# The seven products of the first MLP product in another order

## The chip, the cores and the metric

The kernel runs on one core of a Trainium2 chip. The metric is the device time of one execution in microseconds, as the median of repeated runs. The profile is one more execution, recorded by the hardware profiler; its times count from the start of its span.

## The reference

Inputs are q, k, v of shape (8 batches, 8 heads, 576 tokens, 64) and two MLP weights, all float32 at the interface. First comes attention inside chunks of 64 tokens, then a mixing block over the 512 features of each token:

```python
x   = attention(q, k, v)                  # (8, 576, 512), softmax within chunks of 64 tokens
mix = real(fft(fft(x, axis=1), axis=2))   # Fourier mixing over tokens and features
u   = x + mix
un  = (u - mean(u)) / sqrt(var(u) + 1e-6)
out = u + relu(un @ w_ch1) @ w_ch2        # w_ch1: 512 x 2048, w_ch2: 2048 x 512
```

The two matrix products of the last line are the MLP, and most of the work.

## The kernel before, in words

**Tiling.** Tokens are cut into tiles of 128 and the tiles into nine groups of four (512 tokens): one group for each batch, and a last one for the tokens left over. For each group the MLP runs two stages: the first product (512 features to 2048) with a ReLU, into the buffer `h1`, and the second product (2048 back to 512). Attention, Fourier mixing and normalization for the groups to come are cut into steps, and a loop at the end of the kernel (from line 1190) draws some of these steps each time the MLP yields. So the work of other stages stands between the matmuls of the MLP, on all engines.

**The order is written out.** All of it runs under a manual schedule: on each engine the instructions stand in the order in which the Python code issues them. Each engine works through its own queue in that order. If one waits, everything behind it waits.

**Seven products instead of eight.** From group 2 on, `up_halves` (line 998) computes the first product by a Strassen-Winograd scheme: operands are cut into quarters, and seven products of quarter size replace eight. The 2048 outputs are 16 row blocks of 128; block m of the upper half goes with block HF + m of the lower half (HF = 8). The loop takes two such m at once, a pair of row blocks (r = 0, 1), so a group has four pairs. A pair takes seven turns, one for each product `o`. A turn does product `o` for r = 0 and then for r = 1, with two contraction blocks for each: four matmuls of 128 x 128 weights by 256 columns, each of which shows as two records in the trace. With seven such groups that makes 7 x 4 x 7 x 8 = 1568 records on line 1015. The weights of a turn are one slab of 256 KB, fetched from device memory into a ring of ten slabs; `fetch(1)` asks for one more after each turn.

**Where the products go.** For each row block there are two PSUM tiles, `pa` and `pb`, of 2 x 256 float32 per partition, which is 2 KB: a bank each. They come from the pool `ps_f` with four buffers, so the two row blocks of a pair use all four and the next pair uses the same four again. The products of a row block are put together like this, where P0 to P6 are the products by their index `o`, and `a` and `b` are small buffers in `tmp`:

- P0 into `pa`, first half; ScalarE copies it to `a` (line 1020)
- P1 into `pa`, second half; VectorE makes b = P1 + a (line 1022)
- P2 into `pb`, first half; VectorE makes a = P2 + b (line 1024)
- P3 into `pb`, second half; VectorE writes P3 + a to `h1` (line 1026)
- P4 is accumulated onto P0 in `pa`; ScalarE writes its ReLU to `h1` (line 1030)
- P5 is accumulated onto P2 in `pb`; VectorE adds b (line 1032), ScalarE takes the ReLU (line 1033)
- P6 is accumulated onto P3 in `pb`; VectorE adds b (line 1035), ScalarE takes the ReLU (line 1036)

Indices in this text start at 0. The short name of the change counts differently: the product that it calls P6 is P1 here, the one with `o` = 1.

A matmul that is the first into a fresh bank carries the start flag; the first product into the other half of that bank does not, and the accumulating ones don't either.

**Beside the products.** After P3, `operands` (line 917) prepares sums of the previous pair's outputs for the second product: two VectorE instructions (lines 919 and 920) and one of GpSimd (line 921) for each row block. The function yields after turns 1, 3, 5 and 6 of a pair, and there the loop may put in steps of attention: the exponential and the transpose of q (line 348), the transposes of the probabilities on TensorE (line 329) with that of k on VectorE, or the two small attention products (lines 428 and 380) with the softmax on VectorE (lines 441 to 445, 393 and 395). The loads of q and k for the next tile are issued on the SP queue (line 194), the same queue that issues the slabs (line 910) and the small copies of line 481 to 485.

**The second product** (`down_halves`, line 1043) follows the same scheme with longer products: eight contraction blocks for each product and row block.

Of the kernel before, what the change touches and what calls it, by code (L numbers as in the profile page):

```python
# [11 lines left out]
ALU = mybir.AluOpType  # L12
# [4 lines left out]
def kernel(  # L17
# [32 lines left out]
    nc = tc.nc  # L50
# [46 lines left out]


    NO, HF = 7, KF // 2
    s1 = dram.tile([HF // 2, NO, 128, 2 * 2 * 128], FP32, name="s1")  # L100
    s2 = dram.tile([NO, 128, HF * HM], FP32, name="s2")
    NS1, NS2, Z1, Z2 = 10, 3, 2 * 2 * 128, HF * HM
    slab1 = [wa[:, i * Z1:(i + 1) * Z1].rearrange("p (k r f) -> p k r f", r=2, k=2) for i in range(NS1)]
# [58 lines left out]
    start = one_p.tile([128, KF * 512], FP32, tag="big", name="start")  # L162
# [740 lines left out]
    first_of = {1: 2, 2: 1}  # L903
    n_slab = {1: 0, 2: 0}

    def fetch(which):
        i = n_slab[which]
        if which == 1 and i < HF // 2 * NO * (NG - first_of[1]):
            pair, o = divmod(i % (HF // 2 * NO), NO)
            nc.sync.dma_start(out=slab1[i % NS1].rearrange("p k r f -> p (k r f)"), in_=s1[pair, o])  # L910
        elif which == 2 and i < NO * (NG - first_of[2]):
            nc.sync.dma_start(out=slab2[i % NS2].rearrange("p m e -> p (m e)"), in_=s2[i % NO])
        n_slab[which] = i + 1
# [3 lines left out]
    def operands(h1, m):  # L917

        nc.vector.tensor_tensor(out=xs[:, m], in0=h1[:, m, hi], in1=h1[:, HF + m, hi], op=ALU.add)
        nc.vector.tensor_tensor(out=ys[:, m], in0=xs[:, m], in1=h1[:, m, lo], op=ALU.subtract)  # L920
        nc.gpsimd.tensor_tensor(out=h1[:, m, hi], in0=h1[:, m, lo], in1=h1[:, m, hi], op=ALU.subtract)  # L921
# [76 lines left out]
    def up_halves(g):  # L998
        unT = unTs.pop(g)
        h1 = one_p.tile([128, KF, G * 128], FP32, tag="big", name="h1")  # L1000
        rhs = (unT[:, 0:2, lo], tt[:, 1], tt[:, 0], unT[:, 0:2, hi], unT[:, 2:4, lo], unT[:, 2:4, hi], tt[:, 2])
        for pair in range(HF // 2):
            pas, pbs = {}, {}
            for o in range(NO):
                w = slab1[((g - first_of[1]) * HF // 2 * NO + pair * NO + o) % NS1]
                for r in range(2):
                    m = 2 * pair + r
                    a, b = tmp[:, r, 0], tmp[:, r, 1]
                    if o == 0:
                        pas[r] = ps_f.tile([128, 2, 256], FP32, tag="ff", name="pa")  # L1010
                    if o == 2:
                        pbs[r] = ps_f.tile([128, 2, 256], FP32, tag="ff", name="pb")
                    dst = (pas, pas, pbs, pbs, pas, pbs, pbs)[o][r][:, (0, 1, 0, 1, 0, 0, 1)[o]]
                    for kk in range(2):
                        nc.tensor.matmul(  # L1015
                            out=dst, lhsT=w[:, kk, r], rhs=rhs[o][:, kk],
                            start=(o in (0, 2) and kk == 0), stop=(kk == 1), skip_group_check=True,
                        )
                    if o == 0:
                        nc.scalar.copy(a, dst)  # L1020
                    elif o == 1:
                        nc.vector.tensor_tensor(out=b, in0=dst, in1=a, op=ALU.add)  # L1022
                    elif o == 2:
                        nc.vector.tensor_tensor(out=a, in0=dst, in1=b, op=ALU.add)  # L1024
                    elif o == 3:
                        nc.vector.tensor_tensor(out=h1[:, HF + m, hi], in0=dst, in1=a, op=ALU.add)
                        if pair > 0:
                            operands(h1, m - 2)
                    elif o == 4:
                        nc.scalar.activation(out=h1[:, m, lo], in_=dst, func=ACTF.Relu)  # L1030
                    elif o == 5:
                        nc.vector.tensor_tensor(out=h1[:, m, hi], in0=dst, in1=b, op=ALU.add)  # L1032
                        nc.scalar.activation(out=h1[:, m, hi], in_=h1[:, m, hi], func=ACTF.Relu)
                    else:
                        nc.vector.tensor_tensor(out=h1[:, HF + m, lo], in0=dst, in1=b, op=ALU.add)
                        nc.scalar.activation(out=h1[:, HF + m], in_=h1[:, HF + m], func=ACTF.Relu)
                fetch(1)
                if o in (1, 3, 5, 6):
                    yield h1
        for m in (HF - 2, HF - 1):  # L1040
            operands(h1, m)

    def down_halves(g, h1):
        pas, pbs = {}, {}
        for o in range(NO):
            w = slab2[((g - first_of[2]) * NO + o) % NS2]
            for r in range(2):
# [45 lines left out]
                if r == 1:  # L1093
                    if o == 1:
                        for j in range(0, HF, 2):
                            two = ys[:, j:j + 2]
                            nc.gpsimd.tensor_tensor(
                                out=two, in0=h1[:, HF + j:HF + j + 2, lo], in1=two, op=ALU.subtract
                            )
                    if o == 2:  # L1100
                        for i in range(2):
                            nc.gpsimd.tensor_tensor(
                                out=os_[:, 2 * i + 1, HM:DM], in0=tmp[:, i, 0],
                                in1=natural(groups[g][2 + i])[:, HM:DM], op=ALU.add,
                            )
                    fetch(2)
                yield

    def mlp(g):

        for h1 in up_halves(g) if g >= first_of[1] else up_plain(g) if g > 0 else up_first():
            yield
        yield from (down_halves if g >= first_of[2] else down_plain)(g, h1)

    with tc.manual_schedule():
# [74 lines left out]
        for g in range(NG):  # L1190
            for _ in mlp(g):
# [27 lines left out]
                if t == begin[1] + KF // 2:  # L1219
                    for _ in range(NS2):  # L1220
                        fetch(2)
# [52 lines left out]
```

## Time and profile before

| what | value |
|---|---|
| time, median of 3 runs | 1102.69 us (1102.44 to 1103.81) |
| span of the profiled execution | 1100.7 us, granted TensorE clock 0.999 |
| first product by seven products, seven groups, from start to end | 57.3, 57.1, 57.3, 56.5, 54.9, 48.5, 48.5 us |
| of VectorE's time in these stages, busy | 0.64, 0.69, 0.64, 0.70, 0.60, 0.47, 0.47 |

The stages are those between the first and the last record of line 1015 in each group; in the first five, attention and Fourier steps for later groups stand between the products.

A row of groups reads: line, engine, operation, what is written and what is read, shapes, how many; then after a bar the busy time in us and the mean duration of one in ns; then after a second bar the idle time of the engine just before these instructions, and what ended most of it. A row of waits reads: engine, tile and line that waited, what it waited for, then the total in us, how often, and the longest. A row of the timeline reads: start in us, length in us, engine, line, operation, tiles, shapes, number of instructions merged, and in brackets the idle time before the first of them, with what ended it. PE is TensorE, DVE VectorE, ACT ScalarE, POOL GpSimd; SPq is the queue of the SP engine, which issues most transfers.

Matmuls are pipelined, and their records overlap: one record is longer than the distance from its start to the start of the next. To see how fast TensorE goes, compare starts.

### The profile page before, as it was taken

Reading aid. Unit: us, or ns where it says so; the run is one execution under the profiler, and the core shown is the slowest. Engines: PE = TensorE matmul, PEld = TensorE weight load, DVE = VectorE, ACT = ScalarE, POOL = GpSimd, SP = SyncE. Lnnn points to the kernel's source line nnn. Section 1 sums busy time; section 2 is a strip of 40 time slices with the busy share of each in tenths; the row PEclk is TensorE's granted clock in tenths of the full one; section 3 lists DMA queues with packets and bytes.
Section 4 is the critical chain, followed back from the end, with each engine's and each line's share of the span. In section 5 each row is a group of like instructions: output and inputs, shape, how many; then the busy total and the mean of one; then the engine's idle time right before and its main releaser. Section 6 shows DMA issues by size and latency. Waiting matters only on the chain.

```text
span 1100.7 us, 18766 instructions
## 1 busy us (share of the span) xinstructions
PE 1076.5 (98%) x7016; PEld 847.0 (77%) x7016; DVE 583.0 (53%) x1260; ACT 296.3 (27%) x725; POOL 280.2 (25%) x403
## 2 busy tenths in 40 slices
PE   8999999999999999999999999999999999999998
PEld 6644454447887888888887888888888888888887
DVE  4799987324556355663566455725663534323511
ACT  4688553212112311322022212221123102201200
POOL 4200102354405140243024230424042401220140
PEclk9999999999999999999999999999999999999999
DMA  8767557678567547692668357764743355446232
GB/s 168 234 180 195 152 170 232 186 240 284 191 186 203 152 153 207 188 245 84 199 186 240 96 178 217 204 174 137 205 168 105 117 193 175 127 154 204 82 115 77
DMA packets 147970, 192.73 MB, mean 175 GB/s; under 512 B 66126, under 2 KB 104014, under 8 KB 140712
## 3 DMA queue, kind: packets, MB, share of 16 engines
q1 hardware_dynamic: 145620, 190.20, 57.7%
q8 instruction: 56, 0.92, 0.3%
q0 software_dynamic: 512, 0.68, 0.3%
q10 hardware_dynamic: 1748, 0.66, 0.2%
q14 instruction: 34, 0.28, 0.1%
HBM read 167.22 MB, written 24.12 MB: 174 GB/s over the span
## 4 chain that ended last, share of the span: by engine, by line
PE 83%; DVE 6%; DMA 5%; ACT 3%; SPq 1%; issue 1%; POOL 1%; DVEq 0%; ACTq 0%; POOLq 0%
PE pb L1065 19%; PE pa L1065 15%; PE pb L1015 14%; PE pa L1015 11%; PE dn L969 5%; PE up L948 4%; PE pt L329 3%; PE up L931 2%; PE more_z L648 2%; DMA q<-in_q_dram 2%; PE mix L696 2%; PE z L648 2%; PE xp L428 1%; PE sc L380 1%; DMA k<-in_k_dram 1%
## 5 line engine op out<-in xcount | busy, mean ns | idle before, releaser
L921 POOL TENSOR_TENSOR h<-h 128x256 f32<-128x256 f32 x64 | 56.3, 884 | 274.6 <-PE pb L1015 152.4
L1065 PE MATMUL pa<-wb,h 128*128 128x256 f32 x512 | 115.6, 380 | 0.0
L1065 PE MATMUL pb<-wb,h 128*128 128x256 f32 x512 | 114.9, 379 | 0.0
L1015 PE MATMUL pb<-unT,wa 128*128 128x256 f32 x448 | 107.0, 382 | 5.1 <-DVE wa L1024 4.8
L1015 PE MATMUL pb<-wa 128*128 128x256 f32 x448 | 107.2, 382 | 2.4 <-DVE h L1032 2.4
L1015 PE MATMUL pa<-unT,wa 128*128 128x256 f32 x448 | 106.6, 381 | 0.0
L1065 PEld LDWEIGHTS pa<-wb,h 128*128 128x128 f32 x512 | 96.1, 190 | 13.4 <-issue 0.5
L1065 PEld LDWEIGHTS pb<-wb,h 128*128 128x128 f32 x512 | 96.3, 190 | 12.6
L1015 PEld LDWEIGHTS pb<-unT,wa 128*128 128x128 f32 x448 | 84.0, 190 | 20.8 <-DVE wa L1024 9.7
L1015 PEld LDWEIGHTS pb<-wa 128*128 128x128 f32 x448 | 83.7, 190 | 15.3 <-DVE h L1032 3.6
L1015 PEld LDWEIGHTS pa<-unT,wa 128*128 128x128 f32 x448 | 83.8, 190 | 11.2
L931 PE MATMUL up<-unT,wa 128*128 128x512 f32 x128 | 58.0, 600 | 2.0 <-ACT h L939 1.2
L969 PE MATMUL dn<-wb,h 128*128 128x512 f32 x128 | 57.4, 596 | 1.3 <-ACT h L939 1.3
L1065 PE MATMUL pb<-wb,yall 128*128 128x256 f32 x256 | 58.2, 381 | 0.0
L1065 PE MATMUL pa<-wb,yall 128*128 128x256 f32 x256 | 57.9, 380 | 0.0
L1030 ACT ACTIVATE h<-pa 128x256 f32<-128x256 f32 x56 | 21.5, 384 | 134.8 <-PE pa L1015 134.8
L1065 PE MATMUL pb<-wb 128*128 128x256 f32 x256 | 57.7, 379 | 0.0
L1022 DVE TENSOR_TENSOR wa<-pa,wa 128x256 f32<-128x256 f32 x56 | 23.8, 424 | 63.3 <-PE pa L1015 61.9
L948 PE MATMUL up<-unT,wa 128*128 128x512 f32 x128 | 56.8, 596 | 0.0
L1015 PE MATMUL pa<-wa 128*128 128x256 f32 x224 | 53.4, 381 | 1.5 <-ACT wa L1020 1.5
L1065 PEld LDWEIGHTS pa<-wb,yall 128*128 128x128 f32 x256 | 47.7, 190 | 6.4
L1065 PEld LDWEIGHTS pb<-wb,yall 128*128 128x128 f32 x256 | 47.7, 190 | 6.3
(242 smaller groups left out, 1656.3 us busy)
## 6 DMA issues: line engine op xcount, KB each, us to landing
wb<-s SPq DMA_DIRECT2D x56, 1024.0 KB
wa<-s SPq DMA_DIRECT2D x196, 256.0 KB
xall<-in_moe_w_ch_dram SPq DMA_DIRECT2D x22, 512.0 KB
q<-in_q_dram SPq DMA_DIRECT2D x96, 112.0 KB
k<-in_k_dram SPq DMA_DIRECT2D x96, 112.0 KB
v<-in_v_dram SPq DMA_DIRECT2D x124, 64.0 KB
yall<-in_moe_w_ch_dram SPq DMA_DIRECT2D x10, 512.0 KB
s<-wb SPq DMA_DIRECT2D x20, 256.0 KB
```

Of the source, the lines that this page charges most:

```text
L329: nc.tensor.transpose(pt[:, j, :], src(j), ident)
L380: nc.tensor.matmul(out=sc[t0:t0 + CH, e, j * CH:(j + 1) * CH], lhsT=a[r0:r0 + D, 2 * j + c, 0:CH], rhs=b[r0:r0 + D, 2 * j + c, 0:CH], star ...
L648: nc.tensor.matmul(out=out_, lhsT=lhsT[p], rhs=tk[p, i, T // 2 if T != 5 else 0, cols], start=start, stop=stop, skip_group_check=True,)
L696: nc.tensor.matmul(out=mix[:, cols], lhsT=zt[:, T], rhs=tab, start=(T == 0), stop=(T == 3), skip_group_check=True,)
L921: nc.gpsimd.tensor_tensor(out=h1[:, m, hi], in0=h1[:, m, lo], in1=h1[:, m, hi], op=ALU.subtract)
L931: nc.tensor.matmul(out=up, lhsT=w1[:, kk, m * 128:(m + 1) * 128], rhs=unT[:, kk], start=(kk == 0), stop=(kk == KD - 1),)
L948: nc.tensor.matmul(out=up, lhsT=w1[:, kk, m * 128:(m + 1) * 128], rhs=unT[:, kk], start=(kk == 0), stop=(kk == KD - 1),)
L969: nc.tensor.matmul(out=dn, lhsT=h1[:, m, s * 128:(s + 1) * 128], rhs=w2[:, m, :], start=(m == 0), stop=(m == KF - 1),)
L1015: nc.tensor.matmul(out=dst, lhsT=w[:, kk, r], rhs=rhs[o][:, kk], start=(o in (0, 2) and kk == 0), stop=(kk == 1), skip_group_check=True,)
L1022: nc.vector.tensor_tensor(out=b, in0=dst, in1=a, op=ALU.add)
L1030: nc.scalar.activation(out=h1[:, m, lo], in_=dst, func=ACTF.Relu)
L1065: nc.tensor.matmul(out=dst, lhsT=lhs[:, m], rhs=w[:, m], start=(o in (0, 2) and m == 0), stop=(m == HF - 1), skip_group_check=True,)
```

## The change

The seven products are taken in the order P1, P0, P2, P3, P4, P6, P5 and are spread over the two banks in another way. P1 opens `pb`, P0 opens `pa`; P2 takes the second half of `pa`, P3 the second half of `pb`; P4 is still accumulated onto P0 and P5 onto P2, which both are in `pa` now, and P6 onto P3 in `pb`. The bank of a row block thus goes pb, pa, pa, pb, pa, pb, pa over the seven turns, where it went pa, pa, pb, pb, pa, pb, pb. The aim is that a product does not go into the bank that VectorE is just reading for the product before it. Counted with both row blocks, three products then lie between two into the same bank, except for P0 and P2, which are neighbours.

P1 has no reader of its own any more when it is done: b = P1 + a is made after P0, from the bank of P1 and the copy of P0. The slabs are fetched in the new order. The yields stay where they were, after turns 1, 3, 5 and 6, whatever product is done there.

```diff
+    UP = (1, 0, 2, 3, 4, 6, 5)
...
-            nc.sync.dma_start(out=slab1[i % NS1].rearrange("p k r f -> p (k r f)"), in_=s1[pair, o])
+            nc.sync.dma_start(out=slab1[i % NS1].rearrange("p k r f -> p (k r f)"), in_=s1[pair, UP[o]])
...
-            for o in range(NO):
-                w = slab1[((g - first_of[1]) * HF // 2 * NO + pair * NO + o) % NS1]
+            for turn_, o in enumerate(UP):
+                w = slab1[((g - first_of[1]) * HF // 2 * NO + pair * NO + turn_) % NS1]
...
-                    if o == 2:
+                    if o == 1:
                         pbs[r] = ps_f.tile([128, 2, 256], FP32, tag="ff", name="pb")
-                    dst = (pas, pas, pbs, pbs, pas, pbs, pbs)[o][r][:, (0, 1, 0, 1, 0, 0, 1)[o]]
+                    dst = (pas, pbs, pas, pbs, pas, pas, pbs)[o][r][:, (0, 0, 1, 1, 0, 1, 1)[o]]
...
-                            start=(o in (0, 2) and kk == 0), stop=(kk == 1), skip_group_check=True,
+                            start=(o in (0, 1) and kk == 0), stop=(kk == 1), skip_group_check=True,
...
                     if o == 0:
                         nc.scalar.copy(a, dst)
-                    elif o == 1:
-                        nc.vector.tensor_tensor(out=b, in0=dst, in1=a, op=ALU.add)
+                        nc.vector.tensor_tensor(out=b, in0=pbs[r][:, 0], in1=a, op=ALU.add)
...
-                if o in (1, 3, 5, 6):
+                if turn_ in (1, 3, 5, 6):
                     yield h1
```

More of the change, by code (lines that the diff above doesn't have):

```diff
@@ L1033, in up_halves @@
                         nc.scalar.activation(out=h1[:, m, hi], in_=h1[:, m, hi], func=ACTF.Relu)
-                    else:
+                    elif o == 6:
                         nc.vector.tensor_tensor(out=h1[:, HF + m, lo], in0=dst, in1=b, op=ALU.add)
```

## The prediction

> **What bounds the kernel now.** I read the page's busy line and the chain first, then the groups of the first MLP product (line 1015), then who TensorE waited for, then the timeline.
>
> ```profile
> PE 1076.5 (98%) x7016; PEld 847.0 (77%) x7016; DVE 583.0 (53%) x1260; ACT 296.3 (27%) x725; POOL 280.2 (25%) x403
> ...
> PE 83%; DVE 6%; DMA 5%; ACT 3%; SPq 1%; issue 1%; POOL 1%; DVEq 0%; ACTq 0%; POOLq 0%
> ...
> L1015 PE MATMUL pb<-unT,wa 128*128 128x256 f32 x448 | 107.0, 382 | 5.1 <-DVE wa L1024 4.8
> L1015 PE MATMUL pb<-wa 128*128 128x256 f32 x448 | 107.2, 382 | 2.4 <-DVE h L1032 2.4
> ...
> L1015 PE MATMUL pa<-wa 128*128 128x256 f32 x224 | 53.4, 381 | 1.5 <-ACT wa L1020 1.5
> ```
>
> TensorE is busy 98% and is 83% of the chain that ended last: the time is its stream plus its gaps. The fields after the second bar are the idle time just before a group and what ended it. In line 1015 they sum to 5.1 + 2.4 + 1.5 = 9.0 us. TensorE's waits name the same three:
>
> ```profile
> PE pb L1015 <- DVE wa L1024: 4.8, 8, 0.7
> PE pb L1015 <- DVE h L1032: 2.4, 3, 1.1
> ...
> PE pa L1015 <- ACT wa L1020: 1.5, 4, 0.4
> ```
>
> Line 1024 is the VectorE add that reads product 2, and what waits for it is product 3. Line 1032 reads product 5, and product 6 waits. Line 1020 copies product 0, and product 1 waits. In each case the next product goes into the other half of the same `pa` or `pb`, and starts only when the reader of the first half is done. An undisturbed stretch gives the measure of a turn (one product for both row blocks, 8 records):
>
> ```profile
> 356.32 1.89 PE L1015 MATMUL pb<-unT,wa 128*128 128x256 f32 x8
> 358.05 1.89 PE L1015 MATMUL pb<-wa 128*128 128x256 f32 x8
> 359.77 1.89 PE L1015 MATMUL pa<-unT,wa 128*128 128x256 f32 x8
> 361.50 1.89 PE L1015 MATMUL pa<-wa 128*128 128x256 f32 x8
> ```
>
> Starts lie 1.727 us apart (5.18 us over three), 0.216 us a record. Here is a disturbed pair, first TensorE, then VectorE:
>
> ```profile
> 333.89 1.99 PE L1015 MATMUL pb<-wa 128*128 128x256 f32 x8
> 336.54 1.99 PE L1015 MATMUL pb<-unT,wa 128*128 128x256 f32 x8 [0.65 <-DVE wa L1024]
> 338.37 1.89 PE L1015 MATMUL pa<-unT,wa 128*128 128x256 f32 x8
> 340.09 1.89 PE L1015 MATMUL pb<-unT,wa 128*128 128x256 f32 x8
> 343.09 1.99 PE L1015 MATMUL pb<-wa 128*128 128x256 f32 x8 [1.10 <-DVE h L1032]
> ```
>
> ```profile
> 335.46 0.69 DVE L395 TENSOR_TENSOR ex<-sc,mx 128x512 f32<-128x512 f32 x1
> 336.07 0.74 DVE L1024 TENSOR_TENSOR wa<-pb,wa 128x256 f32<-128x256 f32 x2
> ...
> 341.70 1.07 DVE L348 STREAM_TRANSPOSE qT<-q 128x512 f32<-128x512 f32 x1
> 342.63 0.73 DVE L1032 TENSOR_TENSOR h<-pb,wa 128x256 f32<-128x256 f32 x2
> ```
>
> VectorE is late because softmax, or the operands of line 919 and a transpose, stand ahead of the add in its queue.
>
> **What the Trainium skill says.** "PSUM — Partial Sum Buffer", section "PSUM bank collisions raise a hardware error": two engines on one bank and quadrant collide even at different columns, so semaphores must guard by bank. The trace agrees: product 3 writes the half that nobody reads, and still waits 0.65 us for line 1024. "Perfetto Trace Analysis", section "Matmuls": groups should rotate through different banks, so that one is evacuated under the matmuls of the next; the turn from `pb` to `pa` at 338.37 shows it, with no wait. Same page, "Identifying Dependency Chains": an instruction that waits for several engines can get event-semaphore instructions ahead of it; line 1015 has 135 of them, 51 ns each, on the weight-load queue. "SBUF — State Buffer", section "Who interferes with whom": a VectorE instruction with two SBUF inputs contends with GpSimd reads. Line 919 takes 0.41 us at 366.36, and 0.76 and 0.88 us at 338.05 and 339.88, where GpSimd works.
>
> **The change part by part.**
>
> Step 1, the price of a stall. A stall costs its idle time, plus 0.163 us because the last record before it (0.379 us) isn't overlapped down to 0.216, plus 0.104 us because the first record after it takes 0.320 to the next start instead of 0.216: idle + 0.267. Check: 340.09 to 343.09 is 3.00, less 1.73 is 1.27 = 1.10 + 0.16, and the 0.10 follows.
>
> Step 2, how many. By the starts in the timeline I count 18 stalls, in the five groups that have attention work between their products: idle 0.65, 1.10, 0.74 from 316.6; 0.37, 0.13, 0.37, 0.71, 0.37 from 434.5; 0.65, 1.12, 0.65 from 552.9; 0.12, 0.13, 0.37, 0.38, 0.37 from 670.7; 0.61, 0.19 from 788.6. Sum 9.02 + 18 x 0.267 = 13.8 us. By group: 3.3, 3.3, 3.2, 2.7, 1.3. The last two groups (from 900.7 and 999.1) take 48.5 us each, about 28 turns x 1.727, and have none.
>
> Step 3, what the new order gives. Banks per pair were pa pa pb pb pa pb pb, and become pb pa pa pb pa pb pa. Undisturbed, a reader starts 0.20 us after TensorE has left its row block (line 1032 at 358.25 after the turn at 358.05) and takes 0.37 to 0.42: it is done some 0.6 us after its row block, and the next product wants that bank half a turn, 0.86 us, after it. So neighbours in one bank have 0.24 us of slack. With another product between, it is 0.24 + 1.73 = 1.97 us. VectorE's largest delay now is 1.27 us of stall, so all 14 VectorE stalls fit.
>
> Step 4, the one neighbouring pair left: product 0, then product 2, both `pa`, with the ScalarE copy between. The four ScalarE stalls (0.37 each) came from two ReLUs of line 1036, late behind softmax (463.60 to 465.11), queued ahead of the copy. Now product 1 leads the pair with no reader of its own, so the copy comes one turn (1.73 us) later and its 0.53 us delay vanishes. In the two undisturbed groups the copy causes no wait at all, and the distance is the same now.
>
> Step 5, new waits. The add of line 1022 now waits for the copy too (about 0.4 us later), but the next writer of that bank, product 3, is a turn further on. Product 1 of the next pair waits for the add on product 6, and product 0 for that on product 5, each with one turn between, where three turns or two lay before. Walking the worst pair (572 to 583) through VectorE's queue with the durations shown, the add on product 6 ends some 0.6 us before its bank is wanted. Behind such a waiting matmul stands all of TensorE, so a miss would cost as in step 1. Extra two-semaphore waits: some 20 in TensorE's instruction list and 19 in VectorE's, 20 x 0.051 and 19 x 0.021 us, below 1.5 us if nothing hid them; the 135 of now leave records 0.216 apart, so they hide under matmuls: zero.
>
> Step 6, what an earlier TensorE runs into. Transposes already wait for their loads: k at 346.18 (0.63 us), q at 468.53 (0.51) and 704.17 (0.17). There the SP queue is issuing without a pause after a DMA-to-DMA wait (line 484), so these loads don't come earlier, while TensorE does, by 2.2, 1.7 and 1.4 us. At the first, scores need that k 2.1 us after it was ready: about 0.1 to 0.3 us lost. At the second, the adds on product 2 stand behind the transpose: 0 to 0.9 us, at the third 0 to 0.4. Bounds 0 and 1.6; I take 1.0.
>
> No matmul, byte or VectorE operation is added; slabs are fetched in the new order, one a turn as before. Edits to the slab index and start flags cost nothing: same instructions.
>
> Sum: 1102.7 - 13.8 + 1.0 = 1089.9 us.
>
> **The rivals.** (A) The forecast, 1089.9.
> (B) The stalls move rather than vanish: VectorE is busy 60 to 70% in those groups and an earlier TensorE leaves it less time, so half comes back at the reused banks or the late loads: 1102.7 - 6.9 = 1095.8. For it: the loads of step 6. Against it: VectorE idles between turns (0.89 us before line 1026 at 337.70), so it does not saturate.
> (C) No change: ScalarE's copy becomes the wait that sets the pace: 20 loaded pairs x (0.37 + 0.267) = 12.7 us back, 1101.6. Against it: step 4.
> (D) Slower: the copy, the add behind it and late loads stall every one of the 28 pairs, 28 x (0.37 + 0.267) = 17.8, less 13.8, plus 1.0: 1107.7. For it: copy and add are now chained. Against it: the add's bank is wanted a turn later.
>
> **How the numbers follow.** A 0.80, B 0.13, C 0.03, D 0.04. The range begins at everything gained with no late load (1088.9), less 1 us for the spread of runs (1102.4 to 1103.8), and ends just short of B. A and B are faster by over 0.2%, C is counted as the same though half of it would be faster, D is slower.
>
> **What would show it.** Right: idle before the seven-product matmuls falls from 9.0 to under 1.5 us, nothing from VectorE's readers of `pa` or `pb`; the five loaded groups get shorter by about 3.3, 3.3, 3.2, 2.7 and 1.3 us; the last two keep 48.5. Step 4 is wrong if idle behind the ScalarE copy exceeds 1.5 us, step 5 if product 1 or 0 waits for adds on products 6 or 5, step 6 if transposes of q and k don't wait longer. The prediction is wrong if the stalls go and the span does not, that is, if the second product or the side work then waits on data.

## The result

| | time, us |
|---|---|
| before, median of 5 runs | 1102.69 (1102.18 to 1103.84) |
| changed, median of 5 runs | 1092.11 (1090.95 to 1092.66) |
| ratio, 95% interval | 0.9897 (0.9884 to 0.9911) |

The changed kernel is 10.6 us faster; 12.8 were forecast, and 1092.1 lies inside the range of 1087.9 to 1095.2. Two further comparisons, on two chips, gave 1092.93 beside 1103.92 and 1092.35 beside 1103.32: 11.0 us both times. The ratios, here and below, are not the quotients of the two medians beside them; what is clear of noise is read from their intervals.

### The profile page after: what moved, and what is told of

The parts are those of the page before. It is cut to its first block, busy times and chain, and to the rows that moved or that the text cites. A ratio compares the mean times of both kernels' runs of the same rounds, so it can differ in the third digit from the quotient of the medians.

```text
span 1089.2 us, 18830 instructions
## 1 busy us (share of the span) xinstructions
PE 1071.9 (98%) x7016; PEld 849.2 (78%) x7016; DVE 577.9 (53%) x1260; ACT 298.2 (27%) x725; POOL 281.1 (26%) x403
## 4 chain that ended last, share of the span: by engine, by line
PE 90%; DMA 3%; SPq 2%; ACT 2%; DVE 2%; issue 1%; DVEq 0%; ACTq 0%
PE pb L1065 20%; PE pa L1016 17%; PE pa L1065 15%; PE pb L1016 13%; PE dn L970 5%; PE up L949 4%; PE up L932 3%; PE pt L330 3%; PE more_z L649 2%; PE mix L697 2%; PE z L649 2%; PE xp L429 2%; PE sc L381 1%; DMA yall<-in_moe_w_ch_dram 1%; SPq L195 1%
## 5 line engine op out<-in xcount | busy, mean ns | idle before, releaser
L1016 PE MATMUL pa<-unT,wa 128*128 128x256 f32 x672 | 159.3, 380 | 0.0
L1016 PEld LDWEIGHTS pa<-unT,wa 128*128 128x128 f32 x672 | 126.7, 190 | 17.2
L1022 DVE TENSOR_TENSOR wa<-pb,wa 128x256 f32<-128x256 f32 x56 | 23.5, 423 | 65.4 <-ACT wa L1021 65.4
L1021 ACT COPY wa<-pa 128x256 f32<-128x256 f32 x56 | 20.8, 372 | 125.2 <-PE pa L1016 125.2
L1016 PE MATMUL pb<-unT,wa 128*128 128x256 f32 x224 | 53.0, 379 | 0.0
L714 POOL TENSOR_TENSOR xall<-y,xall 128x513 f32<-128x513 f32 x14 | 21.3, 1518 | 122.3 <-DVE y L708 122.3
```

The lines of the kernel that those rows point to most:

```text
L714: eng.tensor_tensor(out=x[:, 0:w], in0=y[:, 0:w], in1=x[:, 0:w], op=ALU.add)
L1016: nc.tensor.matmul(out=dst, lhsT=w[:, kk, r], rhs=rhs[o][:, kk], start=(o in (0, 1) and kk == 0), stop=(kk == 1), skip_group_check=True,)
L1022: nc.vector.tensor_tensor(out=b, in0=pbs[r][:, 0], in1=a, op=ALU.add)
```

## The profile after

Line numbers are one higher now up to the copy of product 0 (line 1021), so the matmuls of line 1015 stand at line 1016; from the add of line 1022 on they are as before. First the page: TensorE's share and its part of the chain, then the four groups of matmuls that had 9.0 us of idle time ahead of them.

```profile
PE 1071.9 (98%) x7016; PEld 849.2 (78%) x7016; DVE 577.9 (53%) x1260; ACT 298.2 (27%) x725; POOL 281.1 (26%) x403
...
PE 90%; DMA 3%; SPq 2%; ACT 2%; DVE 2%; issue 1%; DVEq 0%; ACTq 0%
...
L1016 PE MATMUL pa<-unT,wa 128*128 128x256 f32 x672 | 159.3, 380 | 0.0
...
L1016 PE MATMUL pb<-wa 128*128 128x256 f32 x448 | 106.6, 381 | 0.0
...
L1016 PE MATMUL pa<-wa 128*128 128x256 f32 x224 | 53.5, 382 | 0.0
L1016 PE MATMUL pb<-unT,wa 128*128 128x256 f32 x224 | 53.0, 379 | 0.0
```

The idle time after the last bar was 5.1, 2.4, 1.5 and 0.0 us and is 0.0 in all four. VectorE has gone from the chain's second place with 6% to 2%. The stretch that answers to the disturbed pair shown in the prediction, first TensorE, then VectorE:

```profile
335.30 1.99 PE L1016 MATMUL pa<-wa 128*128 128x256 f32 x8
337.13 1.89 PE L1016 MATMUL pb<-unT,wa 128*128 128x256 f32 x8
338.86 1.89 PE L1016 MATMUL pa<-unT,wa 128*128 128x256 f32 x8
340.58 1.89 PE L1016 MATMUL pb<-wa 128*128 128x256 f32 x8
342.31 1.89 PE L1016 MATMUL pa<-unT,wa 128*128 128x256 f32 x8
...
349.11 0.69 PE L381 MATMUL sc<-kT,qT 64*64 64x64 f32 x32 [0.39 <-DVE kT L349]
```

```profile
337.54 0.75 DVE L1024 TENSOR_TENSOR wa<-pa,wa 128x256 f32<-128x256 f32 x2
...
342.78 1.10 DVE L349 STREAM_TRANSPOSE qT<-q 128x512 f32<-128x512 f32 x1 [1.39 <-DMA q<-in_q_dram]
343.73 0.73 DVE L1035 TENSOR_TENSOR h<-pb,wa 128x256 f32<-128x256 f32 x2
...
347.93 1.12 DVE L349 STREAM_TRANSPOSE kT<-k 128x512 f32<-128x512 f32 x1 [2.81 <-DMA k<-in_k_dram]
```

Look at line 1024, the add on product 2. It comes at 337.54, later than the start of product 3 (337.13), which would have waited for it before. Now product 3 goes into `pb` and starts on time; only product 4 at 338.86 needs that bank. The softmax is as late as ever, but there is a turn for it. The same with the add on product 6 (line 1035): it starts at 343.73, when product 5 has been running since 342.31.

What has grown is the idle time of VectorE ahead of its transposes of q and k: 1.39 and 2.81 us here. One of them reaches TensorE: the scores at 349.11 wait 0.39 us for the transpose of a k that was late. It is TensorE's only idle time of over 0.1 us from group 2 on. A slab that landed late, at 363.65, left no idle time, but it put off the next turn: the starts of the matmul records around it lie 0.36 and 0.29 us apart instead of 0.22, which cost 0.2 us.

Stage by stage the two profiles can be laid side by side, since undisturbed stages repeat, most of them to 0.02 us:

| profile | group 2 begins at | from there to the end | groups 2 to 6, us |
|---|---|---|---|
| before | 316.6 | 784.1 | 57.34 57.08 57.27 56.50 54.94 |
| changed | 318.0 | 771.1 | 54.85 53.95 54.02 53.80 53.55 |

The last two groups take 48.51 us and the eight stages of the second product the same within 0.02 us in both. So from group 2 on the stream is 13.0 us shorter; but group 2 began 1.4 us later, in a part of the kernel where no line differs.

## The experiments

Besides the times, each kernel gave a profile. TensorE's stream from group 2 on and the stalls in it tell more than the medians do. In the table, after_again and after_third are the changed kernel, before_again is the kernel before, and the others are explained below:

| kernel | time, us | before, same chip | from group 2 on | groups 2 to 6 |
|---|---|---|---|---|
| after_again | 1092.93 | 1103.92 | 773.6 | 55.45 53.80 55.58 54.22 53.55 |
| banks_only | 1093.60 | 1103.92 | 775.1 | 55.94 54.98 55.67 53.95 53.55 |
| order_only | 1103.19 | 1103.92 | 783.5 | 57.37 56.64 57.39 56.03 55.13 |
| worst_banks | 1100.17 | 1103.92 | 782.2 | 57.44 55.84 56.05 55.24 55.58 |
| shift_pool | 1089.56 | 1103.16 | 770.7 | 54.02 53.87 54.02 53.80 53.75 |
| before_shift_pool | 1102.93 | 1103.16 | 783.5 | 57.25 56.25 57.35 56.24 54.93 |
| no_shift | 1088.30 | 1103.16 | 770.4 | 54.02 53.80 54.02 53.80 53.55 |
| before_again | one run, 1103.05 | 1103.16 | 784.5 | 57.36 57.16 57.27 56.78 54.94 |
| after_third | 1092.35 | 1103.32 | 772.4 | 54.91 53.84 55.03 54.03 53.55 |
| shift_pool_2 | 1090.62 | 1103.32 | 770.6 | 54.02 53.80 54.02 53.80 53.75 |
| banks_shift | 1089.26 | 1103.32 | 770.4 | 54.02 53.80 54.02 53.80 53.55 |

### Banks or order?

The change does two things, a new order and a new place for each product. The two halves were run alone. First the banks, with the order of before:

```diff
-                    if o == 2:
+                    if o == 1:
                         pbs[r] = ps_f.tile([128, 2, 256], FP32, tag="ff", name="pb")
-                    dst = (pas, pas, pbs, pbs, pas, pbs, pbs)[o][r][:, (0, 1, 0, 1, 0, 0, 1)[o]]
+                    dst = (pas, pbs, pas, pbs, pas, pas, pbs)[o][r][:, (0, 0, 1, 1, 0, 1, 1)[o]]
...
-                            start=(o in (0, 2) and kk == 0), stop=(kk == 1), skip_group_check=True,
+                            start=(o in (0, 1) and kk == 0), stop=(kk == 1), skip_group_check=True,
```

> The kernel before with the old order of products, P0 to P6, but the banks of the change: P0, P4 and P2, P5 in pa, P1 and P3, P6 in pb. By turns a row block's banks are pa pb pa pb pa pa pb, so the only neighbours in one bank are P4 and P5, with ScalarE's ReLU between. Theory (the wait for a bank that VectorE still reads is the whole loss): no VectorE stall is left, idle before the seven-product matmuls falls from 9.0 to under 1.5 us, and the time is that of the changed kernel within 2 us, 1090 to 1094. Rival (the order matters, since P1 ahead gives the copy of P0 a free turn, and the bank only goes with it): the time stays above 1098.

Measured: 1093.60 us, ratio 0.9913 (0.9901 to 0.9926), with the changed kernel at 1092.93 (0.9904, 0.9890 to 0.9919) on the same chip. The theory holds for the time. Idle time before the seven-product matmuls is 1.5 us, all of it before one kind of matmul:

```profile
L1015 PE MATMUL pa<-unT,wa 128*128 128x256 f32 x672 | 155.1, 380 | 1.5 <-DVE wa L1024 0.9
```

So one stall behind VectorE is left, 0.92 us, against the expectation, and it is of another kind: the add on product 2 stood behind a transpose whose q had come 2.9 us late. A slab that came late cost 0.55 us, and late k's cost the scores 2.0 us.

Then the order alone, starting from the changed kernel:

```diff
-                    if o == 0:
+                    if o == 1:
                         pas[r] = ps_f.tile([128, 2, 256], FP32, tag="ff", name="pa")
-                    if o == 1:
+                    if o == 2:
                         pbs[r] = ps_f.tile([128, 2, 256], FP32, tag="ff", name="pb")
-                    dst = (pas, pbs, pas, pbs, pas, pas, pbs)[o][r][:, (0, 0, 1, 1, 0, 1, 1)[o]]
+                    dst = (pas, pas, pbs, pbs, pas, pbs, pbs)[o][r][:, (0, 1, 0, 1, 0, 0, 1)[o]]
...
-                            start=(o in (0, 1) and kk == 0), stop=(kk == 1), skip_group_check=True,
+                            start=(o in (1, 2) and kk == 0), stop=(kk == 1), skip_group_check=True,
...
-                        nc.vector.tensor_tensor(out=b, in0=pbs[r][:, 0], in1=a, op=ALU.add)
+                        nc.vector.tensor_tensor(out=b, in0=pas[r][:, 1], in1=a, op=ALU.add)
```

> The new order P1, P0, P2, P3, P4, P6, P5, but the banks of before: P0, P4 and P1 in pa, P2, P5 and P3, P6 in pb. Neighbours in one bank with a VectorE reader are then P2 and P3, and P6 and P5, as there were two such places before. Theory: VectorE's stalls stay, 7 to 8 us of idle, and only the four ScalarE stalls of 0.37 us idle go, worth 4 x 0.64 = 2.5 us: 1100 us (1098.5 to 1102). Rival (the order is what helps): 1090 to 1094.

Measured: 1103.19 us, ratio 1.0000 (0.9992 to 1.0008). The order alone gives nothing that the medians show; the 2.5 us that I expected from ScalarE's stalls did not come either. The stream from group 2 on is 0.6 us shorter than before. TensorE's waits in this kernel:

```profile
PE pb L1016 <- DVE wa L1024: 7.1, 11, 1.1
PE pb L1016 <- DVE h L1035: 2.4, 3, 1.1
```

ScalarE is gone from the list, as expected. But behind line 1024 TensorE waits 7.1 us, where the groups of the kernel before show 5.1. Since b is made after the copy of product 0, the two adds of line 1022 come later, and a transpose of q and the add on product 2 are queued behind them: that add starts 1.88 us after the start of product 2 (456.29 after 454.41), against 1.55 in the second profile of before (454.23 after 452.68). The wait that follows grows by the same 0.33 us, from 0.13 to 0.46. The chained copy and add, which the slow rival feared, are real: with 1.9 us more idle time behind line 1024 they cost most of what the earlier copy saved. In the first profile of the full change no wait behind line 1024 is left: there they have a turn to hide in.

A third assignment was meant to be worse than the old one:

```diff
-                    if o == 2:
+                    if o == 1:
                         pbs[r] = ps_f.tile([128, 2, 256], FP32, tag="ff", name="pb")
-                    dst = (pas, pas, pbs, pbs, pas, pbs, pbs)[o][r][:, (0, 1, 0, 1, 0, 0, 1)[o]]
+                    dst = (pas, pbs, pbs, pas, pas, pbs, pas)[o][r][:, (0, 0, 1, 1, 0, 1, 1)[o]]
...
-                            start=(o in (0, 2) and kk == 0), stop=(kk == 1), skip_group_check=True,
+                            start=(o in (0, 1) and kk == 0), stop=(kk == 1), skip_group_check=True,
```

> The old order, P0 to P6, with P3, P6 beside P0, P4 in pa and P2, P5 beside P1 in pb: banks by turns pa pb pb pa pa pb pa, and the next pair begins with pa again. Neighbours with a VectorE reader are P1 and P2, P3 and P4, P6 and the next P0. Theory: the add on P3 for the second row block stands behind the operands of the first (0.8 us, 1.6 beside GpSimd), so P4 stalls in most pairs: some ten pairs at 0.9 + 0.27 us, a dozen at 0.1 to 0.3, and four stalls of about 1.1 us at the next P0 behind the softmax: 15 to 19 us in place of 13.8, so 1104 to 1109 us, and unlike before the two undisturbed groups stall as well and exceed 48.5 us. Rival (the banks are not what counts): 1102.7 as before.

Measured: 1100.17 us, ratio 0.997 (0.9962 to 0.9978). The expectation was wrong by 3.8 us and more, and in direction. Two parts of it came true: TensorE waits for line 1026, and for that alone of VectorE's readers, and the two undisturbed groups lose time now (49.06 us each instead of 48.51).

```profile
PE pa L1015 <- DVE h L1026: 5.0, 8, 1.3
```

Wrong were the count and the size: 8 stalls with idle time, five of them over 0.5 us, instead of ten of 0.9 us and a dozen short ones. And the four stalls of the next product 0 behind product 6 did not come: in group 3 product 0 starts at 465.63, before the adds on product 6 start at 465.98, so it isn't in the bank that they read. I had assumed which bank the pool hands to the next tile, and did not look. The profiled run was the slowest of this kernel's 20 (1103.98), but because its group 2 began at 319.9 us, the latest of all; from there on its stream, 782.2 us, is 1.9 us shorter than before.

In all these kernels a bank is also one tile of the program. So the runs show that the place of a product sets the wait; whether the wait is kept for the bank or for the tile, they do not tell apart.

### Where did the missing 2 us go?

The changed kernel, once more:

> The changed kernel, unaltered, run once more. The recorded pair of profiles shows TensorE's stream 13.0 us shorter from the start of group 2 on, and the part before group 2, where no line differs, 1.4 us longer (group 2 begins at 318.0 us instead of 316.6). Theory (chance): the start of the kernel varies from one execution to the next by about a microsecond, so group 2 begins anywhere between 316 and 318.5 us here, its stages after that repeat within 0.1 us (54.9, 54.0, 54.0, 53.8, 53.6, 48.5, 48.5), and the median lies between 1089.5 and 1092.5. Rival (the change slows the start too): group 2 begins at 318.0 again, and the median is 1092.

> The changed kernel a third time, on the same chip as the two kernels that follow, so that they can be set beside it. Theory (its residue is late loads, which vary): from group 2 on its stream takes between 770.8 and 774 us, and the median is 1091 to 1093.5. Rival: 770.3 to 770.8, and the residue was chance.

The start varies: over all thirteen profiles group 2 begins between 316.6 and 319.9 us, with the changed kernel at 318.0, 317.6 and 317.0 and the kernel before at 316.6 and 316.8. But the expectation that the stages after it repeat was wrong: 771.1, 773.6 and 772.4 us, and the second median, 1092.93, lies above its range, too; the third run came out as expected. What varies is TensorE's waits, all of them for data: in the second profile a transpose of k (1.03 us), a slab (0.66), and an add queued behind a late q (0.16); in the third a k (0.78) and a slab (0.20). Late slabs cost more than this idle time: in the third profile turns of group 2 that waited for a slab (at 337.96, 357.15 and 362.77) came late by 0.25, 0.20 and 0.44 us, by the distances between starts. The slab that was late in the second profile:

```profile
339.50 1.75 PE L1016 MATMUL pa<-unT,wa 128*128 128x256 f32 x7 [0.66 <-DMA wa<-s]
```

The SP queue shows why. This is the changed kernel's first profile, around the late k; the second has the same issues in the same order:

```profile
327.91 1.20 SPq L482 DMA_DIRECT2D first<-xall  x2
329.17 0.59 SPq L483 DMA_DIRECT2D first<-xall  x1
331.71 1.09 SPq L485 DMA_DIRECT2D xall<-first  x2
332.85 0.55 SPq L486 DMA_DIRECT2D xall<-first  x1
333.50 1.95 SPq L911 DMA_DIRECT2D wa<-s  x4
335.49 5.61 SPq L195 DMA_DIRECT2D q<-in_q_dram  x8
341.19 0.84 SPq L911 DMA_DIRECT2D wa<-s  x2
342.13 3.66 SPq L195 DMA_DIRECT2D k<-in_k_dram  x8
```

From 327.9 to 333.4 the queue is taken by six tiny copies of `shift`, and from 329.8 to 331.7 it stands, because the copies back wait until those out have landed. Each moves 2 or 4 KB. Slabs, q and k are queued behind them. The transfers themselves have room: in the second profile the DMA engines were busy 52% from 324 to 346 us, and with the copies moved away, where no load is late, 67%. To test it, the copies went to GpSimd's queue, in one word:

```diff
-        eng = nc.gpsimd if b < 2 else nc.sync
+        eng = nc.gpsimd
```

> The changed kernel with the small copies of shift (two gathers and a row out, two scatters and a row back, for each batch) issued on GpSimd's queue for every batch, not for the first alone, so that SP's queue loses six issues of about 0.5 us and one wait on a landing. In the two profiles of the changed kernel, late loads (a k for the scores, a slab) kept TensorE idle for 0.39 and 1.68 us, and its stream from group 2 on took 771.1 and 773.6 us, where 784.1 - 13.8 = 770.3 was to be had. Theory (what the change gave back is lost to loads that come late because SP's queue issues without a pause around these copies): the stream from group 2 on takes 770 to 771.3 us, VectorE's waits for q and k in groups 2 to 5 fall below half, and the time falls by 0.5 to 3 us against the changed kernel. Rival (the loads are late because transfers are slow, or GpSimd's own queue becomes the wait): no gain, or a loss.

> The changed kernel with the copies of shift left out for all batches but the first two, so that row exchanges of the Fourier step are not made for them; everything else is computed. SP's queue loses the six issues and the wait, and GpSimd gets nothing in their place. Theory: as for the copies on GpSimd's queue, 770 to 771.3 us from group 2 on; if GpSimd's queue costs something, this one shows the gain without it. Rival (transfers are slow): as the changed kernel, 771 to 774 us from group 2 on.

> The kernel before with the same edit, the copies of shift on GpSimd's queue. Theory (in the kernel before, late loads were hidden behind the stalls for a bank): no gain, 1102.5 to 1104.5 beside 1103.9 in the last call, and all 18 stalls are still there, 9.0 us of idle within 0.5. Rival (the late loads cost both kernels alike, apart from the banks): it falls by as much as the changed kernel with this edit does, 1 to 3 us.

> The kernel before, unaltered, for a second profile of it. Theory: group 2 begins anywhere between 316 and 318.5 us, since the start of the kernel varies, and from there on the stream takes 784.1 us within 0.5, with the same 18 stalls, because late loads stay hidden behind them. Rival (the stalls before vary as much as the late loads after): over 1 us off.

Measured: with the copies on GpSimd's queue 1089.56 us, ratio 0.9874 (0.9857 to 0.9891), 770.7 us from group 2 on; without them 1088.30 us, ratio 0.9863 (0.9847 to 0.9879), and 770.4 us. The kernel without them leaves out the row exchanges of six of the eight batches, so it serves to measure and is not a version to use. In both, TensorE has no wait of 0.1 us from group 2 on. VectorE's waits for loads in that part, first in the changed kernel, then with the copies on GpSimd's queue:

```profile
DVE kT L349 <- DMA k<-in_k_dram: 5.4, 2, 2.8
DVE qT L349 <- DMA q<-in_q_dram: 4.2, 4, 1.5
```

```profile
DVE kT L349 <- DMA wa<-s: 0.3, 1, 0.3
```

The SP queue there, to be set beside the one above:

```profile
328.18 3.31 SPq L911 DMA_DIRECT2D wa<-s  x4
331.86 4.99 SPq L195 DMA_DIRECT2D q<-in_q_dram  x8
336.95 1.28 SPq L911 DMA_DIRECT2D wa<-s  x2
338.33 4.11 SPq L195 DMA_DIRECT2D k<-in_k_dram  x8
```

The slabs go out at 328.2 instead of 333.5, and the eight parts of k from 338.3 instead of 342.1. In the kernel before, the same edit gives nothing: 1102.93 us, ratio 0.9998 (0.9990 to 1.0007). Its stalls for a bank are still there, with 7.9 us of idle instead of 9.0: those behind line 1024 shrank by 1.1 us in the profile, since the transposes in front of it came earlier. That was a little more than I expected, and the median does not show it. The second profile of before has the same 18 stalls, with 9.4 us of idle, and 784.5 us.

So late loads cost next to nothing as long as TensorE was stalled for a bank anyway (0.6 to 1.0 us of the stream, nothing that the medians show), and cost 0.7 to 3.2 us of the stream once it was not. That the queue is what makes them late is shown by taking the copies away and by moving them.

### The best version

On one chip the changed kernel was set beside itself with the copies moved, and beside the old order with the new banks and the copies moved.

> The changed kernel with the copies of shift on GpSimd's queue, a second time. Theory: from group 2 on 770.3 to 771 us, 1.5 to 4 us faster than the changed kernel on the same chip, 1088.5 to 1090.5. Rival (the gain in the last call was the chip's): within 1 us of the changed kernel.

> The old order P0 to P6 with the new banks, and the copies of shift on GpSimd's queue. Theory (the bank is all, the order is worth nothing of its own once the loads are early): from group 2 on 770.3 to 771.2 us, and within 1 us of the new order with the same copies. The two neighbours left, P4 and P5, cost nothing, since the ReLU has nothing ahead of it that is late. Rival (the order gives slack that this kernel needs): over 1.5 us slower than the new order, with idle time before P5 or P2.

Measured: 1090.62 us (ratio 0.9888, 0.9871 to 0.9906) and 1089.26 us (0.9876, 0.9861 to 0.9891), with 1092.35 (0.9906, 0.9889 to 0.9923) for the changed kernel; the first of these medians is 0.1 us above its expected range. The streams from group 2 on are 770.6 and 770.4 us, and neither has a wait of 0.1 us. The first two intervals overlap and the streams differ by 0.2 us: once the copies are moved, the new order adds nothing that these runs show. The new banks and the moved copies do all of it, 14.1 us below the kernel before (1103.32). The intervals of the changed kernel with and without the copies moved overlap as well, and the 1.7 us between their medians are not proof by themselves. That moving the copies helps is read from the streams: 770.7, 770.6 and 770.4 us in three profiles with the copies moved, against 771.1, 773.6 and 772.4 us.

## Why the prediction was right

**Step 1, the price of a stall**, held to a tenth. The stages without any wait, as no_shift and banks_shift have them (54.02, 53.80, 54.02, 53.80, 53.55), are 3.32, 3.28, 3.25, 2.70 and 1.39 us shorter than before: 13.9 us, against 13.8 from idle time + 0.267, and group by group 3.3, 3.3, 3.2, 2.7, 1.3. The changed kernel's own first profile, late loads included, has 2.49, 3.13, 3.25, 2.70 and 1.39 us.

**Steps 2 and 3, the 18 stalls and the slack of a turn**, held: idle time behind VectorE's readers went from 7.5 us to 0.0. That it is the bank that counts, and not the order, is shown by running each alone.

**Step 4, ScalarE's copy**, held in the change: no wait behind it. Its reason was half the story. The order alone does free the copy, but the chained add then makes VectorE later, by 0.33 us at the place looked at. And the new banks alone free it just as well, since product 1 no longer follows product 0 into its bank: with the old order, too, no wait behind the copy is left.

**Step 5, new waits**: none appeared. Event semaphores on the matmul line went from 135 to 158, and the records still lie 0.216 us apart, so zero was right.

**Step 6, what an earlier TensorE runs into**, is the term that was too small. The mechanism was right, down to the k at the scores of group 2 (0.1 to 0.3 us forecast, 0.39 measured). I took 1.0 us, with 1.6 as the bound. Three profiles give streams of 771.1, 773.6 and 772.4 us, which is 0.7, 3.2 and 2.0 us over the 770.4 without late loads: 2.0 on average. Not foreseen were late slabs, and that this loss changes from one execution to the next. I had read the waits of one profile of before, in which they were still mostly hidden.

With 13.9 - 2.0 the gain would be 11.9 us; the medians say 10.6 to 11.0. The difference of about 1 us is not clear of noise: 11.9 us is a ratio of 0.989, which lies inside all three intervals. In the profiles it is in the start: the changed kernel's group 2 began at 317.5 us on average over three profiles, that of the kernel before at 316.7 over two. Whether that is chance or the change, five profiles don't tell.

Rival B named what took part of the gain, late loads, but not its size: 2 us, not 6.9. Rival C's copy set the pace in no run. Rival D's chained add showed only with the old banks.

## What to carry to other kernels

Here a product that went into one half of a PSUM bank waited for the engine that read the other half, 14 times behind VectorE. So put products that follow each other into different banks, even if each has a half to itself, and give the reader a turn. Price stalls from the distances between starts, not from idle time alone; here the pipeline's run-down and refill added 0.27 us to each. And before counting on a gain, look at what else is just in time: waits that are hidden behind a stall come out when it goes, and a queue in order, with six tiny copies and one wait in it, held back slabs of 256 KB by about 5 us.

## What the runs showed of the hardware

In the two stretches of the SP queue shown, an issue took 0.4 to 0.8 us with the pauses in between, so that eight parts of one load took 3.7 to 5.6 us to issue; with the DMA engines busy 52% there, and 67% once nothing was late, the queue and not the transfers set when data came. A late slab could put off a turn by 0.2 us without any idle time in the trace. The first part of the kernel, with identical instructions, ended anywhere between 316.6 and 319.9 us, while from there on stages without a wait repeated to 0.02 us, with a few exceptions of 0.1 to 0.2 us.
